# The first MLP matrix issued from ScalarE's DMA queue instead of SyncE's, in a gated attention-and-MLP decode kernel

## The chip, the cores and the metric

The kernel runs on one core of a Trainium2 chip. The metric is device time in microseconds (us), the median of several executions. A core has five engines with instruction queues of their own: TensorE (PE in the profile), VectorE (DVE), ScalarE (ACT), GpSimd (POOL) and SyncE (SP, which issues DMAs and computes nothing). They run independently and wait for one another through semaphores. Transfers from the chip's main memory (HBM) into the core's on-chip memory (SBUF) are made by 16 DMA engines, which are fed by queues: SyncE's queue is q1 in the profile, ScalarE's is q10.

## What is computed

Eight decode rows x (8 x 576) go through an attention block over a key and value cache and through an MLP, and a gate per row mixes the two.

```python
q = (x @ wq).reshape(B, 1, 32, 128)              # wq: 576 x 4096
k = repeat(k_cache[:, :, 6144:8192, :], 2)       # 16 kv heads, last 2048 positions
v = repeat(v_cache[:, :, 6144:8192, :], 2)
a = softmax(q @ k.T * 128**-0.5) @ v             # per batch row and head
a = a.reshape(B, 4096) @ wo                      # wo: 4096 x 576
h = gelu(layernorm(x) @ w1 + b1)                 # w1: 576 x 4608
b = h @ w2 + b2                                  # w2: 4608 x 576
g = sigmoid((x * gate_w).sum(-1))
out = g * a + (1 - g) * b
```

All inputs are bf16. The window of K and of V is 64 MiB each (8 rows x 16 heads x 2048 positions x 128), so the two are most of what is read.

## The kernel before

**Order of work.** The kernel is one list of operations, each with the engine it belongs to, the operations whose results it needs (`deps`), and operations that it must only be issued behind (`after`). A planner puts the list into one fixed order for each engine. On the chip each engine executes its own order strictly; a wait holds up everything behind it in that engine's queue.

**Small loads.** ScalarE issues x (L396, 8 rows), the gate vector in two pieces of 6 and 2 rows (L397), and the MLP bias `b1` (L399, 4 rows). Then it loads an activation table and computes the gate's tanh (L416).

**Weights at the start.** SyncE issues, in this order, the last 64 rows of the query matrix (L402, as 128 pieces of 4 KB), its first 512 rows (L403, 128 pieces of 32 KB), the first 512 rows of the first MLP matrix (L405, 128 pieces of 36 KB) and its last 64 rows (L406, 128 pieces of 4.6 KB). Then come the caches.

**Slots.** K and V are streamed by heads through four slots of SBUF, numbered 0 to 3, of 4 MiB each; one load fills one slot with one head's K or V for all eight rows (L603, 256 pieces of 16 KB). The loads are issued by SyncE in the order K0, K1, K2, V0, K3, V1, K4, V2, K5, V3, a quarter of the output matrix `wo` (into a smaller slot of its own, L723), K6, and so on, ending with `b2` (L732) and the second MLP matrix (L743). They take the slots in turn in the order 1, 2, 0, 3. At the start slot 0 holds the query matrix and slot 3 the first MLP matrix, so K2 waits for the query matmul, and V0 for the first MLP matmul. Later a K load waits until the K or V that was in its slot has been used: K3 (slot 1) for the transposes of K0, V1 (slot 2) for those of K1, K4 (slot 0) for those of K2.

**Start-up chain.** TensorE's order is: transposes of x and of the normalised x (L438), the query matmul (L484 and the helper at L175), a selection matmul (L510), matmuls that make a mask (L760), the first MLP matmul (L527 for the bias, then L484 and L175), then the score matmuls (L659 and L175). Between the query matmul and the selection VectorE evacuates and transposes the query (L499, L504); behind the selection ScalarE scatters it (L520) and GpSimd copies it into block-diagonal form (L614). Behind the MLP matmul ScalarE evacuates (L539, L540), VectorE makes the inner polynomial of the tanh form of GELU (L541, L542, L543), ScalarE takes the tanh (L544), VectorE multiplies and transposes (L545, L546).

**K and V.** For each K, VectorE makes four transposes (L647), two for each of two units; the score matmuls of a unit follow. There are two transpose buffers, so a transpose also waits for the scores two before it. Every four units (two K loads) there is a softmax: maximum (L620), exponential on ScalarE (L624), mask reset (L629), transpose of the probabilities (L631). V is used straight by matmuls (L681). In VectorE's order the first K transpose stands directly behind L543, and L545 and L546 stand between the following ones.

Of the kernel before, what the change touches and what calls it, by code (L numbers as in the profile page):

```python
# [38 lines left out]
class _Plan:  # L39
# [16 lines left out]
    def dma(self, eng, fn, semkey, nbytes, deps=(), name=None, after=(), prio=0):  # L56
        op = _Op(eng, fn, deps, name, self.DMA_ISSUE, after=after, is_dma=True, dma_sem=semkey, nbytes=nbytes, prio=prio)
        op.idx = len(self.all)
        self.all.append(op)
        return op  # L60
# [121 lines left out]
def build_kernel(nc, A_x, A_k_cache, A_v_cache, A_wq, A_wo, B_x, B_w1, B_b1, B_w2, B_b2, gate_w, out):  # L182
# [3 lines left out]
    F = B_w1.shape[1]  # L186
# [23 lines left out]
    with ExitStack() as es:  # L210
# [140 lines left out]
        w1_m = RAW[:, W1O:W1O + 4 * F].rearrange("p (t c) -> p t c", t=4)  # L351
        w1_r = RAW[:, W1O + 4 * F:W1O + 4 * F + F // 2]
# [19 lines left out]
        add, dma = P.add, P.dma  # L372
# [26 lines left out]
        d_b1 = dma("act", lambda e: e.dma_start(b1c, B_b1.rearrange("(c f) -> c f", c=FC)), "b", F * 2, name="d_b1", after=[d_gw])  # L399
# [2 lines left out]
        d_wqr = dma("sp", lambda e: e.dma_start(wq_r, A_wq[512:576, :].rearrange("k (s c) -> (k s) c", s=2)), "wq", 64 * 8192, name="d_wqr")  # L402
        d_wqm = dma("sp", lambda e: e.dma_start(wq_m.rearrange("p t c -> p (t c)"), A_wq[0:512, :].rearrange("(p t) c -> p (t c)", t=4)), "wq", 512 * 8192, name="d_wqm", after=[d_wqr])  # L403
        dwq = [d_wqm, d_wqr]
        d_w1m = dma("sp", lambda e: e.dma_start(w1_m.rearrange("p t c -> p (t c)"), B_w1[0:512, :].rearrange("(p t) c -> p (t c)", t=4)), "w1", 512 * F * 2, name="d_w1m", after=[d_wqm])  # L405
        d_w1r = dma("sp", lambda e: e.dma_start(w1_r, B_w1[512:576, :].rearrange("k (s c) -> (k s) c", s=2)), "w1", 64 * F * 2, name="d_w1r", after=[d_w1m])  # L406
        dw1 = [d_w1m, d_w1r]


# [380 lines left out]
def bass_gated_mix__sliding_block_cached__mixer_channel_mlp__decode_kernel(  # L790
    nc: bass.Bass,
    A_x: bass.AP,
    A_k_cache: bass.AP,
    A_v_cache: bass.AP,
    A_wq: bass.AP,
    A_wo: bass.AP,
    B_x: bass.AP,
    B_w1: bass.AP,
    B_b1: bass.AP,
    B_w2: bass.AP,  # L800
    B_b2: bass.AP,
    gate_w: bass.AP,
    out: bass.AP,
):
    build_kernel(nc, A_x, A_k_cache, A_v_cache, A_wq, A_wo, B_x, B_w1, B_b1, B_w2, B_b2, gate_w, out)
# [28 lines left out]
```

## Time and profile before

| | |
|---|---|
| median of 3 runs | 365.9 us (365.89 to 366.47) |
| profiled execution, span | 364.9 us |
| moved | 154.47 MB, mean 423 GB/s |
| PE busy | 247.1 us (68%) |
| DVE busy | 217.0 us (59%) |
| ACT busy | 39.9 us (11%) |
| POOL busy | 23.3 us (6%) |
| mean granted TensorE clock | 0.846 |

Issue to landing of single loads: 13.0 us for L403, 23.4 for L405, 24.3 for L406; for the 16 K loads 28.1 in the median, for the 16 V loads 33.0.

The span is one execution taken by the hardware profiler; the median is of runs without it. The profile gives, for each engine, how long it was busy; the span in 40 slices of 9.1 us, where a digit is the busy share in tenths; the DMA queues with their packets; and the timeline, in which each row is a start in us, a length in us, the engine, the line of the kernel and the operation, and in brackets the idle time ahead of it with what ended it. A DMA's row in the timeline is its issue, not its transfer. The trace also holds the record of every DMA packet (start, duration, size, queue) and the moments at which each of the 16 DMA engines reports its share of a load as landed.

### The profile page before, as it was taken

To read this page: it belongs to the slowest core of one execution; us is meant where nothing else is said; L and a number is where in the kernel's file an instruction comes from. 1 tells how busy PE (TensorE), PEld (TensorE's weight loads), DVE (VectorE), ACT (ScalarE), POOL (GpSimd) and SP (SyncE) were. 2 spreads that over 40 slices of the span, in tenths; PEclk is the share of its full clock that TensorE was granted. 3 is DMA by queue.
4 is the path that set the end of the run, shared out by engine and by line. 5 is a ranking of instruction groups with operands and counts; after the bars stand their busy time and mean duration, and the time that the engine had idled before them with its cause. 6 is when DMAs were issued, how large, how long until landed. Compare 5 with 4: busy or idle time off the path is not lost.

```text
span 364.9 us, 2626 instructions
## 1 busy us (share of the span) xinstructions
PE 247.1 (68%) x1347; PEld 57.3 (16%) x893; DVE 217.0 (59%) x160; ACT 39.9 (11%) x46; POOL 23.3 (6%) x66
## 2 busy tenths in 40 slices
PE   0355676599486957849297957868396938587776
PEld 0100000122111121202111121202110210102333
DVE  0723999667883757256675657276756667085220
ACT  1012100400310040000400040000400040001100
POOL 7210001000100000001000100001000100000000
PEclk9986599699769986969768986989589968969699
DMA  8999999999999999999999999999999999999996
GB/s 347 432 408 429 431 433 427 408 429 432 429 431 431 436 427 431 433 431 433 428 431 433 424 433 429 431 435 431 433 429 433 433 431 429 431 431 431 426 428 263
DMA packets 10674, 154.47 MB, mean 423 GB/s; under 512 B 764, under 2 KB 932, under 8 KB 1320
## 3 DMA queue, kind: packets, MB, share of 16 engines
q1 hardware_dynamic: 10608, 154.29, 99.1%
q8 instruction: 8, 0.13, 0.1%
q10 hardware_dynamic: 56, 0.03, 0.0%
q14 instruction: 2, 0.02, 0.0%
HBM read 154.31 MB, written 0.01 MB: 423 GB/s over the span
## 4 chain that ended last, share of the span: by engine, by line
DMA 66%; DVE 21%; PE 10%; issue 1%; ACT 1%; SPq 0%; DVEq 0%
DMA arena<-in_A_k_cache_dram 59%; DVE arena L647 20%; DMA arena<-in_B_w_dram 7%; PE ps L175 5%; PE ps L659 2%; PE ps L681 2%; DVE arena L546 1%; DVE arena L620 1%; ACT ps L629 1%; PE ps L563 0%; DVE arena L545 0%; PE ps L633 0%; DVE arena L777 0%; PE ps L622 0%; SPq L406 0%
## 5 line engine op out<-in xcount | busy, mean ns | idle before, releaser
L647 DVE STREAM_TRANSPOSE arena<-arena 128x2048 f32<-128x2048 f32 x64 | 144.1, 2289 | 61.8 <-DMA arena<-in_A_k_cache_dram 40.6
L175 PE MATMUL ps<-arena 128*128 128x512 bf16 (+2 forms) x454 | 135.0, 449 | 0.0
L659 PE MATMUL ps<-arena 128*128 128x512 bf16 x128 | 57.7, 451 | 52.5 <-DVE arena L647 52.5
L681 PE MATMUL ps<-arena 128*32 128x512 bf16 x512 | 60.3, 390 | 2.6 <-DVE arena L635 1.9
L624 ACT ACTIVATE arena<-ps,arena 128x2048 bf16<-128x2048 f32 x8 | 15.7, 1967 | 240.5 <-DVE arena L623 240.5
L659 PEld LDWEIGHTS ps<-arena 128*128 128x128 bf16 x128 | 14.0, 109 | 171.9 <-DVE arena L647 114.6
L681 PEld LDWEIGHTS ps<-arena 128*32 128x32 bf16 x512 | 25.2, 99 | 46.1 <-issue 20.3
L620 DVE TENSOR_REDUCE arena<-ps 128x1 f32<-128x2048 f32 x8 | 18.3, 2287 | 12.5 <-PE ps L175 12.4
L614 POOL COPY arena<-arena 32x128 bf16<-32x128 bf16 x32 | 9.2, 288 | 211.3 <-PE ps L175 201.5
L631 DVE STREAM_TRANSPOSE arena<-arena 128x2048 bf16<-128x2048 bf16 x8 | 18.3, 2292 | 6.4 <-ACT arena L624 6.4
L691 DVE SCALAR_TENSOR_TENSOR arena<-ps,arena 128x512 f32<-128x512 f32 x8 | 6.0, 751 | 19.8 <-PE ps L681 19.8
L563 PE MATMUL ps<-arena 128*8 128x288 bf16 (+1 forms) x140 | 12.6, 339 | 6.9 <-DVE arena L706 5.6
L700 PE MATMUL ps<-arena 128*128 128x256 f32 x16 | 5.8, 444 | 16.0 <-POOL arena L696 16.0
L633 PE MATMUL ps<-arena 128*128 128x1 f32 x16 | 4.6, 359 | 15.0 <-ACT ps L629 14.2
L629 ACT ACTIVATE ps<-arena 128x2048 f32<-128x2048 f32 x7 | 13.1, 1876 | 0.1
L696 POOL TENSOR_TENSOR arena<-arena 128x256 f32<-128x256 f32 x8 | 4.9, 612 | 111.3 <-DVE arena L623 63.3
L438 PE MATMUL ps<-arena 8*128 8x8 bf16 x8 | 0.6, 171 | 14.7 <-DVE arena L412 9.6
L694 DVE TENSOR_REDUCE arena<-arena 128x128 f32<-128x512 f32 x8 | 8.4, 1048 | 0.3
L563 PEld LDWEIGHTS ps<-arena 128*8 128x8 bf16 (+1 forms) x140 | 6.4, 97 | 13.5 <-DVE arena L706 7.0
L703 ACT ACTIVATE arena<-ps,arena 64x256 bf16<-64x256 f32 x8 | 3.7, 465 | 43.1 <-PE ps L700 43.1
L706 DVE STREAM_TRANSPOSE arena<-arena 128x256 bf16<-128x256 bf16 x4 | 2.5, 634 | 9.8 <-ACT arena L703 9.8
L541 DVE TENSOR_TENSOR arena<-arena 128x1152 f32<-128x1152 f32 x1 | 1.4, 1359 | 10.5 <-ACT arena L539 10.5
(88 smaller groups left out, 66.2 us busy)
## 6 DMA issues: line engine op xcount, KB each, us to landing
arena<-in_A_k_cache_dram SPq DMA_DIRECT2D x16, 4096.0 KB, 28.1
arena<-in_A_v_cache_dram SPq DMA_DIRECT2D x16, 4096.0 KB, 33.0
arena<-in_B_w_dram SPq DMA_DIRECT2D x1, 4608.0 KB, 23.4
arena<-in_A_wo_dram SPq DMA_DIRECT2D x4, 1152.0 KB, 34.7
arena<-in_A_wq_dram SPq DMA_DIRECT2D x1, 4096.0 KB, 13.0
arena<-in_B_w_dram SPq DMA_DIRECT2D x2, 1728.0 KB, 27.3
arena<-in_B_w_dram SPq DMA_DIRECT2D x1, 1152.0 KB, 26.7
arena<-in_B_w_dram SPq DMA_DIRECT2D x1, 576.0 KB, 24.3
```

The source lines that it names most:

```text
L175: return e.add_instruction(mybir.InstMatmult(name=nc.get_next_instruction_name(), engine=mybir.EngineType.PE, ins=[e.lower_ap(rhs), e.lowe ...
L563: ins = e.matmul(ps[32 * j:32 * j + 8, BK_ACC, 0:JN], lhsT, rhs[:, JN * j:JN * j + JN], start=False, stop=True, skip_group_check=True, til ...
L614: return e.tensor_copy(dst, src)
L620: mx = add("dve", lambda e: e.tensor_reduce(out=k(MX), in_=ps[:, 0:4, :].rearrange("p a n -> p (a n)"), axis=AXL.X, op=ALU.max), deps=[qk_ ...
L624: ex = add("act", lambda e: e.activation(out=Pm, in_=ps[:, 0:4, :].rearrange("p a n -> p (a n)"), func=ACTF.Exp, bias=k(NB), scale=SCALE, ...
L629: mask_done[g + 1] = add("act", lambda e: e.activation(out=ps[:, 0:4, :].rearrange("p a (n c) -> p (a n) c", c=4), in_=bass.AP(arena_f, of ...
L631: pt_done[g] = add("dve", lambda e: e.transpose(bass.AP(arena, offset=aoffs("PT") + 2048 * (g % 2), ap=[[AST, 128], [8, 64], [512, 4], [1, ...
L647: tr = add("dve", (lambda h=h, kb=kb: lambda e: e.transpose(bass.AP(arena_f, offset=foffs("KT") + kb * 2048, ap=[[AST // 2, 128], [1, 2048]]),
L659: mm = e.matmul(*args, start=False, stop=True, skip_group_check=True) if rc == 0 else held_matmul(nc, e, *args, stop=True, skip=True)
L681: mm = e.matmul(ps[c:c + 32, BK_OS[g % 2], :], PT[:, g % 2, 16 * c + 32 * t:16 * c + 32 * t + 32], slot(s)[:, (j % 2) * SE + 512 * t:(j % ...
L691: vmul = add("dve", lambda e: e.scalar_tensor_tensor(out=vmv, in0=ps[:, BK_OS[g % 2], :].rearrange("p (r d) -> p r d", r=4), scalar=rr[:, ...
L694: acc_ev[g] = add("dve", lambda e: e.tensor_reduce(out=EV[:, g % 2, :], in_=vm.rearrange("p (r d) -> p d r", r=4), axis=AXL.X, op=ALU.add) ...
```

## The change

The two loads of the first MLP matrix are issued by ScalarE instead of SyncE, behind the bias load. The semaphore that the MLP matmul waits for, the places in SBUF and everything else stay. The order of instructions on TensorE, VectorE and GpSimd is the same; ScalarE's queue has two DMA issues more between L399 and the table load of L416; SyncE's has K0 directly behind the query matrix.

```diff
-        d_w1m = dma("sp", lambda e: e.dma_start(w1_m.rearrange("p t c -> p (t c)"), B_w1[0:512, :].rearrange("(p t) c -> p (t c)", t=4)), "w1", 512 * F * 2, name="d_w1m", after=[d_wqm])
-        d_w1r = dma("sp", lambda e: e.dma_start(w1_r, B_w1[512:576, :].rearrange("k (s c) -> (k s) c", s=2)), "w1", 64 * F * 2, name="d_w1r", after=[d_w1m])
+        d_w1m = dma("act", lambda e: e.dma_start(w1_m.rearrange("p t c -> p (t c)"), B_w1[0:512, :].rearrange("(p t) c -> p (t c)", t=4)), "w1", 512 * F * 2, name="d_w1m", after=[d_b1])
+        d_w1r = dma("act", lambda e: e.dma_start(w1_r, B_w1[512:576, :].rearrange("k (s c) -> (k s) c", s=2)), "w1", 64 * F * 2, name="d_w1r", after=[d_w1m])
```

## The prediction

> **What bounds the kernel now.** I read the 40 slices and the table of DMA queues first.
>
> ```profile
> DMA  8999999999999999999999999999999999999996
> GB/s 347 432 408 429 431 433 427 408 429 432 429 431 431 436 427 431 433 431 433 428 431 433 424 433 429 431 435 431 433 429 433 433 431 429 431 431 431 426 428 263
> q1 hardware_dynamic: 10608, 154.29, 99.1%
> q10 hardware_dynamic: 56, 0.03, 0.0%
> ```
>
> Queue q1 (SyncE's) occupies the 16 DMA engines for 99.1% of the span; q10 (ScalarE's) carries only small loads. In the records of single DMA packets one packet follows the other on an engine without a gap, so the time is the sum of the packets, and the only way to lose time is to let the queue run empty. So the question is when each load is issued, and how much is still queued then. The timeline of SyncE's queue comes next (start, length, engine, line):
>
> ```profile
> 1.22 0.42 SPq L403 DMA_DIRECT2D arena<-in_A_wq_dram  x1
> 1.70 0.42 SPq L405 DMA_DIRECT2D arena<-in_B_w_dram  x1
> 2.16 0.43 SPq L406 DMA_DIRECT2D arena<-in_B_w_dram  x1
> ...
> 32.48 0.60 SPq L603 DMA_DIRECT2D arena<-in_A_v_cache_dram  x1
> 49.71 0.60 SPq L603 DMA_DIRECT2D arena<-in_A_k_cache_dram  x1
> 58.55 0.60 SPq L603 DMA_DIRECT2D arena<-in_A_v_cache_dram  x1
> 76.52 0.60 SPq L603 DMA_DIRECT2D arena<-in_A_k_cache_dram  x1
> 77.64 0.60 SPq L603 DMA_DIRECT2D arena<-in_A_v_cache_dram  x1
> ```
>
> From 32.48 on these are V0, K3, V1, K4, V2. By the landing records the load ahead of each lands (last engine) at: K2 56.7, V0 66.5, K3 76.4, V1 86.2, K4 96.3. The reserve at an issue is the difference: 24 us for V0, 17 for K3, 18 for V1, only 9.7 for K4, 19 for V2. K4 is the tight one. What sets its issue is in the timeline of all engines:
>
> ```profile
> 16.13 0.62 PE L484 MATMUL ps<-arena 128*32 128x512 bf16 x4
> ...
> 27.18 1.14 PE L527 MATMUL ps<-arena 4*128 4x384 bf16 x3
> ...
> 32.48 1.13 ACT L539 ACTIVATE arena<-ps 128x1152 f32<-128x1152 f32 x1 [5.03 <-PE ps L175]
> 33.65 1.36 DVE L541 TENSOR_TENSOR arena<-arena 128x1152 f32<-128x1152 f32 x1 [10.52 <-ACT arena L539]
> ...
> 37.31 2.31 DVE L647 STREAM_TRANSPOSE arena<-arena 128x2048 f32<-128x2048 f32 x1
> ...
> 71.98 4.50 DVE L647 STREAM_TRANSPOSE arena<-arena 128x2048 f32<-128x2048 f32 x2 [3.27 <-PE ps L175]
> ```
>
> The query matmul starts at 16.13, the first MLP matmul at 27.18; its end releases ScalarE at 32.48; VectorE then does the three GELU steps L541 to L543, and the first K transpose stands behind them in its queue (37.31). From there VectorE is busy without a DMA wait to 63, and the last transpose of K2 ends at 76.48: it frees slot 0 and lets K4 go at 76.52.
>
> **The change, part by part.** *Bytes and issue cost.* The same bytes move, so no packet time is saved. ScalarE issues two more DMAs (0.42 + 0.43 by the SyncE rows). Behind them stands its table load (2.33, 1.28 us), whose first user starts at 11.54, released by VectorE: some 7 us of cover; without it 0.9 us would fall on the start-up arithmetic. SyncE issues K0 and K1 some 0.9 us earlier, behind the query matrix: nothing.
>
> *The query matrix lands later.* How two queues share an engine is shown by the small loads. On an engine busy with 32 KB query packets (1.21 to 1.23 us each), q10's packets start at 4.83 (gate), 6.09 (its semaphore), 7.36 (second gate piece), 8.61 (semaphore), 9.83 (bias), 11.13 (semaphore): one per query packet, strictly in turn, a 4-byte semaphore write counting as one. Each engine has eight query packets and now eight 36 KB MLP packets (1.37). Where no small load is ahead, the query's semaphore is written after 3.45 + 8 x 1.23 + 8 x 1.37 = 24.2; with 0.4 to landing (last query packet ended 13.80, landed 14.23), 24.6. If the MLP packets come one or two turns late (the gate's issue at 1.41 gave a packet only at 4.83), 23.2. I take 24.0, against 14.2. Lower end: the MLP queue stays out until the query is through, 14.2.
>
> *The chain behind it.* Before, the query matmul waited for the start-up arithmetic (16.13), not the matrix. From its start to the end of the mask matmuls (25.76 + 1.49 = 27.25) is 11.1 us; from 24.0 that ends at 35.1 (34.3 to 36.0).
>
> *The last rows of the MLP matrix land later still.* On the two engines that carry x, both gate pieces and the bias, MLP packets begin only after the bias semaphore's turn, about 12.4. The eight of them alternate with the last query packet, its semaphore and then K0's 16 KB packets (0.61): about 28.0. The semaphore and the eight 4.6 KB packets (0.18) of L406 each pay a K0 packet: 0.6 + 8 x 0.79 + 0.6, so about 35.2 with landing. The same counting gives the old loads 0.3 to 0.5 too early for the last engine: 35.6, against 26.5.
>
> *The MLP matmul* needs both: it starts at about 35.8 instead of 27.18, 8.6 later. It keeps its 5.3 us (27.18 to 32.44), so the GELU steps and the K transposes behind them move by 8.6 as well. VectorE has no idle stretch there to absorb it.
>
> *Which issues survive.* V0 at 41.1 (K2 queued to 56), K3 at 58.3 (V0 to 66), V1 at 67.2 (K3 to 76): covered. K4 moves from 76.52 to 85.1. A first packet comes about 1.0 after an issue into an idle queue (0.79 to 1.80 for L402; 0.74 for the output), so at 86.1. V1 lands on twelve engines by 85.1, on two by 85.3, on the last two at 86.04 and 86.22; less the 0.4 to landing they run dry at 84.5 to 84.9, 85.6 and 85.8. Twelve engines idle about 1.5 us, the last one 0.3.
>
> *What reaches the end.* Between 0.3 and 1.6. Instruction loads (16 KB on q8, at 90.2, 130.6, 173.7 and so on) each put one engine back by about 0.9, and the spread of a landing stays 1.3 to 1.7 up to the last one; so engines that are early now set the end later, and I stay near the upper bound: 1.3. K4 lands 1.3 late at 97.6, ahead of VectorE, which is 8.6 late. The next idle VectorE stretch (5.5 us before 115.64, waiting for K5) begins to absorb the delay, and the reserves after K4 were all over 15 us, so there is one gap only.
>
> *Sum.* 364.9 + 1.3 = 366.2 of span; the median of the runs (365.9) lies 1.0 above the profiled span, so 367.2.
>
> The Trainium skill speaks against the change (DMA: Bandwidth & Descriptors, Rules for kernel authors): spreading DMAs over issuing engines does not help bandwidth, since all run on the same 16 engines and interleave. The alternating small packets agree; by it a gain has no source beyond issue time.
>
> **The rivals.**
> 1. *The queue does not run empty: no change, 365.9.* The delay of K4 must stay under about 7.5 us. For it: the reserve and the delay are nearly equal, and TensorE's clock can help; the query matmuls ran at 0.43 us a step up to 20.6 and would gain 2 us at the 0.22 us of later ones. Against it: the last MLP rows hold the start at 35.6 however fast the query is. A different sharing does it too: if an engine empties one queue's whole load before turning, the query lands at 14.2 and the MLP matrix near 26, as now. Against that: the strict turns above. The Trainium skill (same page, Queues, rings and completion order) has an engine drain a packet of typically 9 to 17 descriptors before it switches, which is this sharing if both MLP loads fit in one turn; the records show one descriptor per turn.
> 2. *The delay is larger: 368.8.* The MLP matmul wholly at half clock lasts 1.0 + 15 x 0.32 = 5.8 instead of 5.3, and the score matmuls ahead of K2's last transpose, at 0.22 a step from 72.98 on, cost 1.1 more at the 0.43 of those before them. 8.6 + 0.5 + 1.1 = 10.2 of delay, 1.6 above the forecast's: loss 1.3 + 1.6 = 2.9. For it: the clock was granted at 0.5 through most of both stretches before, so it follows PE's idle times, and these move. Against it: only one of the two need hit.
> 3. *Faster: about 365.0.* The engines' idle time between first and last packet is what two queues could fill. It adds up to about 1.2 us as a mean over 16 engines, most of it ahead of the output; nothing shows that the first queue left any.
>
> **How the numbers follow.** Forecast 0.54, rival 1 0.24, rival 2 0.17, rival 3 0.05. The forecast's own range is 366.3 (only the last engine's loss) to 368.2 (another microsecond of delay). For 8 in 10 I reach to no change on the low side and nearly to rival 2: 365.8 to 368.9. Noise is about 0.2% (0.7 us; the runs span 365.89 to 366.47). Slower by more: 0.51 of the forecast and all of rival 2, 0.68. Within: rival 1 and 0.03, 0.27. Faster: 0.05.
>
> **What would show it.** The query matmul at 23 to 25; the first MLP matmul at 35 to 36.5, released by the DMA or just behind the mask matmuls; the first K transpose near 46; K4's issue at 84.5 to 86 and a hole in the DMA share just after, the only one; every later landing shifted by the same amount. I am wrong if the query still starts at 16, if K4 leaves before 84, or if the DMA share has no hole and the time differs all the same.

## The result, and the profile after

The changed kernel takes 368.49 us in the median (367.89 to 370.9, 5 runs), against 365.9 (365.61 to 366.47): a ratio of 1.0084, with a 95% interval of 1.0057 to 1.0111. It is slower, as forecast, but by 2.6 us instead of 1.3. Its profiled execution spans 368.4 us, 3.5 more than the one before; the runs themselves spread over 3 us, and the profiled one is the second longest of the five.

The slices and the queue table of the page after the change:

```profile
DMA  8999999996999999999999999999999999999996
GB/s 350 427 414 438 425 431 427 434 427 270 426 423 434 423 436 429 432 431 427 433 434 431 429 436 429 429 429 431 434 436 431 425 438 425 432 429 429 429 428 253
q1 hardware_dynamic: 10320, 148.98, 94.8%
q10 hardware_dynamic: 344, 5.34, 3.4%
```

The MLP matrix has moved to q10. In the row of the DMA engines one slice, the tenth (82.9 to 92.1), falls to 6 tenths and 270 GB/s. At 430 GB/s that slice of 9.2 us would have moved 160 GB/s x 9.2 us = 1.5 MB more, which takes 3.4 us at that rate: practically the whole difference stands in this slice.

The timeline of SyncE's queue after, from V0 on (V0, K3, V1, K4, V2):

```profile
41.61 0.60 SPq L603 DMA_DIRECT2D arena<-in_A_v_cache_dram  x1
58.63 0.60 SPq L603 DMA_DIRECT2D arena<-in_A_k_cache_dram  x1
67.47 0.60 SPq L603 DMA_DIRECT2D arena<-in_A_v_cache_dram  x1
85.93 0.60 SPq L603 DMA_DIRECT2D arena<-in_A_k_cache_dram  x1
87.15 0.60 SPq L603 DMA_DIRECT2D arena<-in_A_v_cache_dram  x1
```

All five are 8.9 to 9.5 later than before. Windows of 1 us around K4's issue (busy us of PE, weight load, DVE, ACT, POOL, the granted clock, the DMA share, GB/s) show the hole. A packet counts in the window in which it starts, so windows without a hole show shares somewhat below or above 1:

```profile
83.00:84.00 1.00, 1.00 (x9) 0.29 (x8) 0.84 (x2) 0.00 (x0) 0.00 (x0) 1.00 0.92 393
84.00:85.00 1.00, 1.00 (x12) 0.43 (x10) 1.00 (x1) 0.00 (x0) 0.00 (x0) 1.00 0.08 33
85.00:86.00 1.00, 1.00 (x12) 0.50 (x10) 0.90 (x1) 0.00 (x0) 0.00 (x0) 1.00 0.00 0
86.00:87.00 1.00, 1.00 (x12) 0.30 (x6) 0.00 (x0) 0.00 (x0) 0.00 (x0) 1.00 0.00 0
87.00:88.00 1.00, 1.00 (x7) 0.19 (x2) 0.00 (x0) 0.00 (x0) 0.00 (x0) 1.00 0.91 262
```

In the kernel before, the change from V1's packets to K4's falls into the same stretch, and no window is empty:

```profile
84.00:85.00 1.00, 0.81 (x4) 0.19 (x2) 1.00 (x2) 0.00 (x0) 0.00 (x0) 1.00 1.11 475
85.00:86.00 1.00, 1.00 (x6) 0.00 (x0) 1.00 (x1) 0.00 (x0) 0.00 (x0) 1.00 1.15 492
86.00:87.00 1.00, 0.78 (x4) 0.10 (x1) 1.00 (x2) 0.00 (x0) 0.00 (x0) 1.00 0.76 328
```

In the packet records after the change, 14 of the 16 engines finish V1's packets at 84.0 to 84.4 and the other two at 84.9 and 85.5; K4's first packets start at 87.3. In between the engines stand still. And the chain that leads to the issue, from the timeline of all engines after the change:

```profile
23.64 0.62 PE L484 MATMUL ps<-arena 128*32 128x512 bf16 x4 [7.62 <-DMA arena<-in_A_wq_dram]
...
33.17 1.48 PE L175 MATMUL ps<-arena 128*128 128x512 bf16 x3
...
35.54 1.13 PE L527 MATMUL ps<-arena 4*128 4x384 bf16 x3 [0.88 <-DMA arena<-in_B_w_dram]
...
41.62 1.13 ACT L539 ACTIVATE arena<-ps 128x1152 f32<-128x1152 f32 x1 [6.75 <-PE ps L175]
...
46.24 2.31 DVE L647 STREAM_TRANSPOSE arena<-arena 128x2048 f32<-128x2048 f32 x1
...
83.59 2.31 DVE L647 STREAM_TRANSPOSE arena<-arena 128x2048 f32<-128x2048 f32 x1 [0.16 <-PE ps L175]
```

The brackets name what ended each wait. TensorE now waits 7.62 us for the query matrix, is through with the mask matmuls at 34.65, and then waits 0.88 for the MLP matrix: its last rows landed at 35.49. The first K transpose is at 46.24 instead of 37.31, the last of K2 ends at 85.90, and K4 goes at 85.93.

### The profile page after: what moved, and what is told of

It reads as the page before. It is cut to its first block, busy times and chain, and to the rows that moved or that the text cites. A ratio compares the mean times of both kernels' runs of the same rounds, so it can differ in the third digit from the quotient of the medians.

```text
span 368.4 us, 2626 instructions
## 1 busy us (share of the span) xinstructions
PE 248.4 (67%) x1347; PEld 57.3 (16%) x893; DVE 217.5 (59%) x160; ACT 39.9 (11%) x46; POOL 23.2 (6%) x66
## 4 chain that ended last, share of the span: by engine, by line
DMA 56%; DVE 20%; PE 20%; issue 2%; ACT 1%; ACTq 0%; DVEq 0%
DMA arena<-in_A_k_cache_dram 40%; DVE arena L647 17%; DMA arena<-in_B_w_dram 16%; PE ps L175 10%; PE ps L681 4%; PE ps L659 4%; DVE arena L620 1%; ACT ps L629 1%; DVE arena L546 1%; PE ps L563 0%; PE ps L484 0%; DVE arena L541 0%; DVE arena L545 0%; PE ps L633 0%; ACT arena L539 0%
## 5 line engine op out<-in xcount | busy, mean ns | idle before, releaser
L175 PE MATMUL ps<-arena 128*128 128x512 bf16 (+2 forms) x454 | 137.1, 458 | 0.0
L681 PEld LDWEIGHTS ps<-arena 128*32 128x32 bf16 x512 | 25.1, 99 | 46.7 <-issue 20.6
L620 DVE TENSOR_REDUCE arena<-ps 128x1 f32<-128x2048 f32 x8 | 18.3, 2286 | 12.5 <-PE ps L175 12.4
L484 PE MATMUL ps<-arena 128*32 128x512 bf16 (+1 forms) x40 | 5.9, 575 | 7.6 <-DMA arena<-in_A_wq_dram 7.6
```

The costliest lines, as they stand in the source:

```text
L175: return e.add_instruction(mybir.InstMatmult(name=nc.get_next_instruction_name(), engine=mybir.EngineType.PE, ins=[e.lower_ap(rhs), e.lowe ...
L620: mx = add("dve", lambda e: e.tensor_reduce(out=k(MX), in_=ps[:, 0:4, :].rearrange("p a n -> p (a n)"), axis=AXL.X, op=ALU.max), deps=[qk_ ...
L681: mm = e.matmul(ps[c:c + 32, BK_OS[g % 2], :], PT[:, g % 2, 16 * c + 32 * t:16 * c + 32 * t + 32], slot(s)[:, (j % 2) * SE + 512 * t:(j % ...
```

## The experiments

The theory is the forecast's: K4 is issued after the queue has run empty, and nothing else costs time. "The hole" is this empty stretch, given as idle time per DMA engine (the mean over 16). The rivals are: (A) two queues on the same engines cost DMA rate; (B) the late start-up chain is never caught up; (C) the last rows alone, or (D) the late query matrix alone, make the loss. Where a run adds work, its result is overwritten or unused.

**The changed kernel again: e1, and the single runs e9, e10 and e11** (no edit).

> The changed kernel unaltered, for a second profile and more times. Theory (the load of K4 is issued after the queue has run empty; how late depends on TensorE's clock): median near 368.5 us with runs spread over 2 us or more; in the profile K4's issue moves away from 85.93 by up to 1.5 us, and the hole in the DMA share and the span move by the same amount, span minus 364.9 being within 0.6 of hole length. Rival A (two queues on the same engines cost DMA rate): the excess over before is the same in each run, and the hole does not account for it. Rival B (the late start-up chain is never caught up and still shows at the tail): the excess follows the start-up chain, not the hole.

> The changed kernel again, for a further profile. From the runs so far the span is 364.7 us as long as K4 is issued by 82.4, and 282.3 us more than K4's issue after that. Theory (TensorE's clock makes the spread between runs): the query matmul starts at 23.5 to 23.7 and the MLP matmul at 35.5 to 36.1 in every profile, but K4's issue differs with the time at which the clock goes to full, between 84 and 87, and the span follows the line within 0.5. Rival (the DMA side makes the spread): K4 is issued at 85.9 to 86.1 each time, and spans differ all the same.

> As for the first look: query at 23.5 to 23.7, MLP matmul at 35.5 to 36.1, span on the line 282.3 plus K4's issue within 0.5.

> As for the first look: query at 23.5 to 23.7, MLP matmul at 35.5 to 36.1, span on the line 282.3 plus K4's issue within 0.5.

e1 took 369.69 us (369.56 to 369.85, ratio 1.0099 [1.0084, 1.0113]), the single runs 369.54, 369.41 and 369.94. K4's issue was at 86.08, 85.85, 85.53 and 86.22, with spans of 368.6, 368.3, 368.2 and 368.7, all within 0.5 of the line stated for the single runs. The holes are 3.1, 3.1, 2.8 and 3.3 us, so in every profile the hole carries all but 0.3 to 0.6 us of the loss. The expected spread did not show: four further profiles lie within 0.7 us of K4's issue, so whether TensorE's clock makes a spread was not put to the test. What made the first five runs span 366.5 to 369.6 stays open. e1's median is also 1.2 above the 368.5 that was expected. Over all twelve runs of this kernel the median is 369.6 and nine lie above 369, so the usual loss is nearer 3.7 us than the 2.6 of the first five. One of the runs missed its expectation in a useful way. In e9 the query matmul started at 22.32, 1.3 early, and the MLP matmul at 35.42 all the same:

```profile
22.32 0.62 PE L484 MATMUL ps<-arena 128*32 128x512 bf16 x4 [6.28 <-DMA arena<-in_A_wq_dram]
...
35.42 1.14 PE L527 MATMUL ps<-arena 4*128 4x384 bf16 x3 [1.55 <-DMA arena<-in_B_w_dram]
```

The mask matmuls were 0.8 early too (31.98 for their first row against 32.77), and the wait ahead of L527 is longer by 0.7: the last rows decide.

**e2: the first two K transposes ahead of the GELU steps in VectorE's queue** (with the changed queues).

```diff
                 trs.append(tr)
+                if n == 1:
+                    o_u2.after.append(tr)
```

> The changed kernel with the first two K transposes ahead of the GELU steps in VectorE's queue (the later ones between them). Theory: about 3.5 to 4.5 us of the delay of 9.4 goes, K4's issue at about 82, first packet at about 83.2 while V1 runs to 84: no hole or under 0.5 us, time 365.7 to 366.6. Rival A: the queues are shared as before, so 368.5 stays. Rival B: the MLP is no earlier, so 367.5 to 368.5.

366.11 us in the median (365.78 to 368.73; ratio 1.002 [1.0003, 1.0036]), K4's issue at 82.96, with a hole of only about 0.3 us. The order of one queue takes all but 0.2 us of the loss away in the median while both DMA queues stay as the change left them, so rival A falls, and the MLP, which is no earlier here, does not cost by itself. Four of the twelve runs lie at 367.2 to 368.7, and the profiled execution (span 366.3) is one of them: the last of its DMA engines is 2.6 us behind the first from K4 to the last load, where the kernel before shows 1.6.

**e3: 43 matmuls on zeros in TensorE's idle times before the MLP matmul.**

```diff
+        def warm(n, ahead_of):
+            def fn(e):
+                mm = None
+                for k in range(n):
+                    args = (ps[:, BK_H + k % 2, :], zeros_bf, maskR)
+                    mm = e.matmul(*args, start=True, stop=True, skip_group_check=True) if k == 0 else held_matmul(nc, e, *args, start=True, stop=True, skip=True)
+                return mm
+            pe = P.order["pe"]
+            pe.insert(pe.index(ahead_of), _Op("pe", fn, [], "warm", 0.1))
+
+        for n, op in ((20, o_qp), (8, o_selp), (5, o_mask0), (10, o_hp)):
+            warm(n, op)
```

> The changed kernel with 43 matmuls on zeros more in TensorE's idle times ahead of the first MLP matmul, so that this runs at full clock (about 2.9 us instead of 5.8). Theory: the MLP matmul still starts at 35.5 (last rows), but ends near 38.5; K4's issue at about 83; hole under 1 us, time 365.9 to 366.9 and less spread. Rival A: 368.5. Rival B: about 366.5 as well (it does not tell B apart).

368.20 us (366.8 to 368.37; ratio 1.0054 [1.0041, 1.0067]), outside the expectation. The query's end came 2.1 earlier and the MLP matmul began at 35.56 as expected, but the clock fell back to half within it:

```profile
36.15 0.35 PE L484 MATMUL ps<-arena 128*32 128x384 bf16 x4
...
38.09 0.54 PE L484 MATMUL ps<-arena 128*32 128x384 bf16 x4
```

So ScalarE got its result at 40.27, 1.35 earlier than in the changed kernel instead of 3, and K4 went at 84.70, 1.2 earlier. The span came down by 1.5 with it. The clock's share of the loss is real, but this edit removed only part of it.

**e4, e8 and e12: the kernel before, with six, three or nine useless multiplications (1.36 us each) on VectorE behind L543.** The MLP loads are on SyncE's queue. L545 moves ahead of the first transpose, and V's evacuation a few places among the transposes of K3.

```diff
+        o_pad = o_v
+        for k in range(6):
+            pad = bass.AP(arena_f, offset=foffs("KT"), ap=[[AST // 2, 128], [1, FCW]])
+            o_pad = add("dve", (lambda pad=pad: lambda e: e.tensor_tensor(out=pad, in0=u_sb, in1=u_sb, op=ALU.mult))(), deps=[o_pad], name="pad%d" % k, cost=1.3, prio=20)
...
-                deps = [d] + ([qk_half[n - 2]] if n >= 2 else [o_selp])
+                deps = [d] + ([qk_half[n - 2]] if n >= 2 else [o_selp, o_pad])
```

> The kernel before with both MLP loads on SyncE's queue, and six multiplications of 1.36 us more (8.3 us in all) on VectorE between the GELU steps and the first K transpose. Theory: the delay alone does it: K4's issue near 85, a hole of 1 to 2 us, time 366.5 to 368.5. Rival A: with one queue there is no loss, 365.9. Rival B: a loss near that of the change.

> The kernel before with three multiplications more (4.2 us) on VectorE ahead of the first K transpose. The runs so far put the point from which K4's issue costs time at about 82.7. Theory: K4's issue at 80.5 to 82, no hole, 365.6 to 366.5. If the delay of the K chain costs time by itself (rival B): 367 to 368.

> The kernel before, all loads on SyncE's queue but the small ones, with nine multiplications more (12.5 us) on VectorE ahead of the first K transpose. Theory: K4's issue at 88.5 to 90, hole of 6 to 7 us behind V1, span on the same line, 370.8 to 372.3 (time about 372 to 373.6). Rival (part of the loss comes from sharing the engines between two queues): clearly below the line.

| useless work | K4's issue | idle per DMA engine behind V1 | span | time |
|---|---|---|---|---|
| 4.2 us (e8) | 80.19 | none | 364.7 | 366.09 (365.87 to 369.0), ratio 1.0027 [1.0006, 1.0048] |
| 8.3 us (e4) | 85.41 | 2.6 us | 367.7 | 369.35 (369.0 to 371.18), ratio 1.0098 [1.0082, 1.0115] |
| 12.5 us (e12) | 89.81 | 5.8 us | 372.2 | 373.68, one run |

K4's issue in e8 was 0.3 earlier than expected, and e12's hole a little shorter than the 6 to 7 us. With one queue the same delay makes the same hole. The windows of e4 (columns as above):

```profile
83.00:84.00 1.00, 1.00 (x14) 0.42 (x10) 1.00 (x2) 0.00 (x0) 0.00 (x0) 1.00 0.92 393
84.00:85.00 1.00, 1.00 (x12) 0.48 (x10) 1.00 (x1) 0.00 (x0) 0.00 (x0) 1.00 0.16 66
85.00:86.00 1.00, 1.00 (x14) 0.40 (x8) 0.39 (x1) 0.00 (x0) 0.00 (x0) 1.00 0.00 0
86.00:87.00 1.00, 1.00 (x8) 0.17 (x2) 0.00 (x0) 0.00 (x0) 0.00 (x0) 1.00 0.45 131
```

4.2 us of delay leave no hole and the median within 0.2 us; 8.3 and 12.5 move K4 by 8.9 and 13.3 from its 76.52 and cost 3.0 and 7.5 us of span over 364.7, which is what lies beyond about 6. That is a threshold, so rival B falls as an account of these profiles and of the median of e8; the four runs of e8 at 367.6 to 369.0 have no profile and are not explained. No part of the loss needs the second queue, so rival A falls again. e4's loss was larger than expected (369.35 against at most 368.5); why is accounted for below.

**e5: only the last rows on ScalarE's queue. e6: only the main rows.**

```diff
-        d_w1m = dma("act", lambda e: e.dma_start(w1_m.rearrange("p t c -> p (t c)"), B_w1[0:512, :].rearrange("(p t) c -> p (t c)", t=4)), "w1", 512 * F * 2, name="d_w1m", after=[d_b1])
-        d_w1r = dma("act", lambda e: e.dma_start(w1_r, B_w1[512:576, :].rearrange("k (s c) -> (k s) c", s=2)), "w1", 64 * F * 2, name="d_w1r", after=[d_w1m])
+        d_w1m = dma("sp", lambda e: e.dma_start(w1_m.rearrange("p t c -> p (t c)"), B_w1[0:512, :].rearrange("(p t) c -> p (t c)", t=4)), "w1", 512 * F * 2, name="d_w1m", after=[d_wqm])
+        d_w1r = dma("act", lambda e: e.dma_start(w1_r, B_w1[512:576, :].rearrange("k (s c) -> (k s) c", s=2)), "w1", 64 * F * 2, name="d_w1r", after=[d_b1])
```

That is e5, against the changed kernel; e6 moves the last rows' DMA in the finished order:

```diff
         P.schedule()
+        P.order["act"].remove(d_w1r)
+        P.order["sp"].insert(2, d_w1r)
```

> Only the last 64 rows of the MLP matrix (0.56 MB) on ScalarE's queue, its main part back on SyncE's behind the query matrix. Theory: the query lands at about 15.5, still ahead of the start-up arithmetic, both MLP loads by 26.5; the chain is where it was, K4's issue at 76 to 77.5, no hole, 365.6 to 366.3. Rival A (sharing itself costs DMA rate): a small part of the loss, since a tenth of the bytes is shared.

> Only the main part of the MLP matrix on ScalarE's queue, its last 64 rows on SyncE's between the query matrix and K0. Theory: the MLP load is complete at about 29, the query still lands near 23.5; the MLP matmul now starts straight behind the mask matmuls at about 34.8 instead of 35.54, K4's issue about 0.7 earlier than in the changed kernel, the loss smaller by about 0.8: 367.5 to 369.2. If the last rows alone made the loss (rival C): no hole, 365.9.

e5: 365.97 us (365.63 to 367.86; ratio 1.0013 [0.9999, 1.0027]). The query landed at 15.30, the MLP rows at 26.6, K4 went at 77.42, without a hole. e6: 367.95 (367.2 to 369.07; ratio 1.0057 [1.0041, 1.0073]). The MLP rows were all there at 26.9 and the MLP matmul followed the mask matmuls at once:

```profile
34.55 1.14 PE L527 MATMUL ps<-arena 4*128 4x384 bf16 x3
```

That is 0.99 earlier than in the changed kernel; K4 went at 85.01, 0.92 earlier, and the span fell by 1.0. So rival C falls: the late query matrix alone makes most of the loss (2.5 of the 3.5 us of span), and the last rows add about 1 us.

**e7: ScalarE issues the MLP loads only when the query matrix has landed.**

```diff
-        d_w1m = dma("act", lambda e: e.dma_start(w1_m.rearrange("p t c -> p (t c)"), B_w1[0:512, :].rearrange("(p t) c -> p (t c)", t=4)), "w1", 512 * F * 2, name="d_w1m", after=[d_b1])
+        d_w1m = dma("act", lambda e: e.dma_start(w1_m.rearrange("p t c -> p (t c)"), B_w1[0:512, :].rearrange("(p t) c -> p (t c)", t=4)), "w1", 512 * F * 2, name="d_w1m", deps=dwq, after=[d_b1])
```

> ScalarE issues the MLP loads only when the query matrix has landed (14.2), still on its own queue. Theory: the query matmul starts at 16.1 as in the kernel before and the mask matmuls end at 27.3, but the MLP packets then alternate with K0's and K1's smaller ones: last rows land near 39.4, K4's issue near 90, hole about 7 us, 371.5 to 374. Rival D (the late query matrix makes the loss): no loss, 365.9 to 366.3.

375.67 us (374.9 to 375.89; ratio 1.0261 [1.0248, 1.0275]), the slowest kernel of the study. The query matmul was on time, and TensorE then waited 14 us for the MLP matrix:

```profile
16.26 0.62 PE L484 MATMUL ps<-arena 128*32 128x512 bf16 x4
...
41.38 1.14 PE L527 MATMUL ps<-arena 4*128 4x384 bf16 x3 [14.18 <-DMA arena<-in_B_w_dram]
```

With the query on time the loss is larger, because the MLP loads are issued later and their packets alternate with K0's and K1's: the last rows land at 41.33 instead of 35.49. So rival D as stated for this run, that an early query is enough, falls. How much the late query costs in the changed kernel is what e6 shows, not this run. Landing at 41.33 was 1.9 later than I had counted, K4 went at 91.82, and the time lies above the expected range. There are two holes, 7.3 us per engine behind V1 and 1.4 behind V0, since K3's reserve was used up too.

## Why the prediction was wrong in size, step by step

The profiles lie on one line: an early K4's issue costs nothing (364.7 to 364.9 at 76.52, 77.42 and 80.19), and a late one gives a span of K4's issue plus 282.3. The two meet at 82.4, which is worked out and not measured: no profile but e2's lies between 80.2 and 84.7. (e7, 91.82: 374.1 measured, 374.1 by the line; e12, 89.81: 372.2 and 372.1; after, 85.93: 368.4 and 368.2; e3, 84.70: 366.9 and 367.0. e2's profile alone is 1 us above, with its late DMA engine.)

*The mechanism was right.* The query was to start at 23 to 25 (23.64), the MLP matmul at about 35.8 (35.54), waiting for the last rows on the engines that carry the small loads; the K transposes 8.6 later (8.9); V0, K3 and V1 covered, one hole ahead of K4, nothing further on. The strict turns hold in kind: the query landed on two engines at 16.6 to 16.8, on two at 19.1 to 19.3, on eleven at 21.8 to 22.1 and on the last at 23.6, that is in steps of whole MLP packets and earliest where the small loads kept these back longest; the MLP's last rows landed on twelve engines at 32.4 to 32.9, on two at 34.0 and on two at 35.2 to 35.5.

Two of these hits hold some luck. The first MLP packets came at 7.1 to 7.5 on eleven engines, two packets later than the count assumed, so on eleven engines the query was there at 21.8 to 22.1 and not at 24 (the prediction had allowed for 23.2); the start of 23.64 hangs on the one engine at 23.6, and e9, which has none so late, started at 22.32. And for the last rows the prediction's own terms, 28.0 + 0.6 + 8 x 0.79 + 0.6, give 35.5 even without the landing, not 35.2; the rows landed at 35.2 to 35.5.

*The step that failed is the size of the hole*, "Twelve engines idle about 1.5 us" and the 1.3 made of it. In the profiled execution an engine idles for 3.1 on average and loses 0.4 more in restarting. Three terms were mis-sized and one was missing:

- K4's issue at 85.93 instead of 85.1: 0.8. "It keeps its 5.3 us" was wrong: the MLP matmul ran wholly at half clock (0.32 us a step; ScalarE released 6.08 after its start instead of 5.3), so that in spite of its slightly earlier start the K transposes are 8.9 late instead of 8.6; from there to the last transpose of K2 (9.4 late) another 0.5 went, in two of VectorE's waits for TensorE: 0.69 instead of 0.48 ahead of L623 in the softmax, and 0.16 ahead of K2's last transpose, where there was none. The clock was granted at 0.5 from 72.14 to 82.38 there, against 65.62 to 72.45 before. This is rival 2's mechanism, in part.
- "A first packet comes about 1.0 after an issue": for a K load into an empty queue it is 1.40, in all ten profiles with a hole of over 1.5 us (1.39 to 1.41). The 1.0 came from a DMA of half as many rows. 0.4.
- "They run dry at 84.5": by the same reckoning, 0.4 ahead of the landing, the first engine ran dry at 83.9 (V1 lands on it at 84.28, 84.91 before). The reserve was read from an execution in which V0 and K3 took 9.9 and 10.05 us on an engine; in the changed kernel, in e4 and in e8 they take 9.72. 0.6.
- The first packet of K4 on an engine takes 0.8 to 1.0 us in the mean of a profile instead of 0.61 (0.91 here), and some later ones are longer too: 0.4 per engine. This term was missing.

1.3 + 0.8 + 0.4 + 0.6 + 0.4 = 3.5, the profiled difference. The median of the first five runs shows 0.9 less than that, and the median of all twelve 0.2 more; the difference between runs is not explained.

*The rivals.* Rival 1 (queue not empty) had its threshold at 7.5 us of delay; the runs put it at 6 (82.4 against 76.5). The other sharing, a queue's whole load in one turn, is ruled out by the query landing at 23.6 and not at 14.2. Rival 2 named the half clock, which was one of four causes, and a time (368.8) close to the median, mostly for other reasons. Rival 3, a gain, did not show: no kernel here is below 365.6 in any run. ScalarE's table load starts at 3.25 instead of 2.33 and its first user no later than before (11.36 against 11.54), so it cost nothing, as forecast; neither did SyncE's earlier issues, as far as shows.

*No version beats the kernel before.* With the queue never empty the time is the sum of the packets; e2 and e5 only come back to it. A gain would need less packet time, which no run here tried.

## What to carry to other kernels

In a kernel that is bound by DMA, read for each load the time between its issue and the end of the load ahead of it; the smallest of these reserves (here 6 us, for a single load) is what any delay upstream may use. Giving two needed-early loads a queue each made the one needed first 9.4 us late (23.6 instead of 14.2) and the other no earlier (its main rows 28.6 instead of 25.1, its last rows 35.5 instead of 26.5), since the engines take turns packet by packet: put what is needed first alone ahead, and count small packets too, each of which pays one large packet of the other queue. A reserve read from one execution was 0.6 us off here, and the time from issue to first packet belongs to it; where delay and reserve are within a microsecond or two of each other, give a range as wide.

## What was not expected

- Issue to first packet into an empty queue is 1.40 us for the 256-row load, with a spread of 0.02 over ten profiles, against 1.0 for the 128-row load at the start; after it, the longest of the engines' first packets takes 0.9 to 1.3 us instead of 0.61.
- Kernels without a hole have single late runs: e5 has three of ten at 367.3 to 367.9, e8 four of nine at 367.6 to 369.0, while the kernel before stays within 365.6 to 366.9 in 22 runs beside them. e2, with a hole of 0.3 us, has four of twelve, and in the one profile of such a run a DMA engine lags. The cause was not looked into.
- Keeping TensorE busy up to about 2 us before a matmul did not keep the clock up for it: in e3 it fell back 1.6 us into the MLP matmul (0.17 us a step until 37.1, 0.32 after).
